# Even frequency classes from gathered rows of U, x copies on GpSimd, and earlier loads in the last pair

## The chip, the cores and the metric

The kernel runs on one NeuronCore of a Trainium2 chip. The metric is the device time of one execution in microseconds (us). TensorE, VectorE, ScalarE, GpSimd and SyncE appear in the profile as PE, DVE, ACT, POOL and SP; PEld is TensorE's weight load.

## The reference

Eight sequences x of 5696 rows and 128 channels are convolved with a filter h along the rows (by a Fourier transform of length 2S = 11392). The result goes through a spectral mix: of its transform of length S the lowest 64 modes are multiplied by complex 128x128 matrices, turned back and added; then u + relu(u @ w_ch) is returned.

```
L = 2 * S
y = irfft(rfft(x, n=L, axis=1) * rfft(h, n=L, axis=0), n=L, axis=1)[:, :S, :]
X = rfft(y, axis=1);  Xm = X[:, :64]
Y[:, :64] = einsum('bmd,mde->bme', Xm, w_r + 1j*w_i)
u = y + irfft(Y, n=S, axis=1)
out = u + maximum(u @ w_ch, 0)
```

## The kernel before, in words

A row number is written as 64 q + p, with q from 0 to 88 and p from 0 to 63. A transform over q (`a_tile`, 32 tiles a pair) gives 90 frequency classes k (`NK`) for each p; a second one over p within each class (`second`) gives 64 frequencies of the long transform per class, real and imaginary parts on the 128 partitions. Batches are worked in four pairs, g_ from 0 to 3 (`NP`). Pairs 1 and 2 are called the middle pairs here.

The classes of a pair are worked in 23 ticks of four (`NT`, `KT`; `tick`, L619). In tick t:

- PE makes the second transform of tick t into two PSUM banks. In pairs 1 to 3 an odd tick makes its own and the next one's (`twin`, L564).
- ACT copies the two banks to SBUF as f16 (`copied`, L557, tile Xs), and DVE multiplies them with the filter's transform Hs to U (`products`, L586). U holds the two products of both batches, 2048 elements a partition, in three rooms used in turn (`NU`). In a straight tick (`straight`, L567: t % 4 == 3 after pair 0) DVE reads PSUM itself, and ACT makes no copy.
- Two ticks later (`LC`) PE turns U of tick t-2 back over p with the constant matrices W1 and W2, in two halves, ACT evacuates each to Z, and SP stores Z to DRAM (zscr, 256 KB).
- Three ticks later (`LM`) PE adds up the low modes from Z of tick t-3 in PSUM bank 7 (`MB`): for each class and batch a matmul with Z as weights and a slice of the constant G as moving operand. An odd class gives all 128 mode rows, an even one two or four columns only, because frequency 2m of the long transform is mode m of the short one.

Z has 6 rooms in pair 0, 10 in pairs 1 and 2, and 8 in the last (`NZS`); a store that has not landed keeps its room. Meanwhile GpSimd issues loads of the next pair's x (`x_load`, L353, eight pieces, one every second tick, into the space that As has left), and DVE copies each into the padded tile Xin (`x_place`, L360). After the ticks come the evacuation of the modes (L696 to L699) and the remaining a_tiles of the next pair, whose first six are woven into the last ticks (`border`) and which need all eight pieces of Xin.

In the last pair GpSimd issues what the last stage needs, at ticks listed in `early` (L529): the mixing weights W in four pieces, two constants (S4, IB), and the stored Z of the first blocks (ZT0 to ZT2). Then the mix, and per block of rows: the back transform over the classes (matmuls on ZT), the modes' part (IBs, C), evacuation to UT, the product with WI = [w_ch, identity], relu (L831), addition (L832) and the store.

The order on each engine is the order in which the program records its operations (`Recorder.add`, L55). Waits follow from tokens: `reads` wait for a token's writer, `writes` and `after` for its writer and its readers. A transfer stands in the queue of the engine that issues it (`dma`, L316), and each ring has so many transfers in flight at once.

Of the kernel before, what the change touches and what calls it, by code (L numbers as in the profile page):

```python
# [4 lines left out]
P = 128  # L5
# [118 lines left out]
def bass_long_conv_fft__then__afno_spectral_mix_kernel(nc, x, h, moe_w_r, moe_w_i, moe_w_ch, out):  # L124
# [12 lines left out]

    qq = np.arange(NQ)
    pp = np.arange(J)
    kk = np.arange(NK)  # L140
    fwd = np.exp(-2j * np.pi * np.outer(qq, kk) / (2 * NQ))
    f1 = np.zeros((P, 2 * NK))
    f1[0:NQ] = np.stack([fwd.real, fwd.imag], axis=2).reshape(NQ, 2 * NK)
    mat = np.exp(-2j * np.pi * (pp[:, None, None] * kk[None, :, None] / L + pp[:, None, None] * pp[None, None, :] / J))
    strip = np.stack([-mat.imag, mat.real, mat.imag], axis=2).reshape(J, NK * 3 * J)
    MW = NK * 3 * J + J
    mt = np.zeros((P, MW))
    mt[0:J, 0:NK * 3 * J] = strip
    mt[J:P, J:MW] = strip
    th = 2.0 * np.pi * np.outer(pp, pp) / J  # L150
    c, s = np.cos(th), np.sin(th)
    w1 = np.block([[c, s], [-c, -s]])
    w2 = np.block([[-s, c], [-s, c]])
# [25 lines left out]
    for k in range(0, NK, 2):  # L179
# [2 lines left out]
        ge += [g[:, k, ri * M + m] for m in ms for ri in range(2)]  # L182
        at_e += 2 * len(ms)
    assert at_e == P
    g = np.concatenate([np.stack(ge, axis=1)] + [g[:, k] for k in range(1, NK, 2)], axis=1)

    def const(name, a):
# [6 lines left out]
    c_ib = const("cIB", ib.reshape(P, -1)[:, 0:SH])  # L194
    c_sg = nc.inline_tensor(np.ascontiguousarray(sg.astype(np.float32)), name="cSG")
    c_g = const("cG", g)
    wd = nc.dram_tensor("wscr", [P, 2 * M * D], F16, kind="Internal")
    zs = nc.dram_tensor("zscr", [NP * NK * P, 2 * D], F16, kind="Internal")

# [26 lines left out]
    a_g = take(HW * 2)  # L226
    g_sb = at("G", GW, F16, a_g)
    ah_sb = at("Ah", HW, F16, a_g)
    NU, NXS, NZ, NZX = 3, 2, 6, 10
    NZS = [NZ] + [NZX] * (NP - 2) + [8]  # L230
    NZL = NZS[-1]
    a_st = take((2 * NU + NXS + NZ) * 2048)
    h_in = at("Hin", J * D, F16, a_st)
# [5 lines left out]
    XB = XN * D  # L239
    x_all = at("Xr", 2 * XC * XB, F16, a_h)  # L240
    x_st = [at(f"Xt{i}", XB, F16, a_as + i * XB * 2) for i in range(2 * XC)]
    u_s = [at(f"U{i}", 2048, F16, a_st + i * 4096) for i in range(NU)]
    x_s = [at(f"Xs{i}", 1024, F16, a_st + NU * 4096 + i * 2048) for i in range(NXS)]
    z_s = [at(f"Zs{i}", 1024, F16, a_st + NU * 4096 + (NXS + i) * 2048) for i in range(NZ)] + \
          [at(f"Zt{i}", 1024, F16, a_g + GW * 2 + i * 2048) for i in range(NZX - NZ)]
# [1 line left out]
    wc_sb = at("Wc", 2 * P, F16, take(2 * P * 2))  # L247
    sg_sb = at("SG", 3, F32, take(12))
    XTW = 3 * M
    xt = at("XT", B * XTW, F16, a_g + GW * 2 + 2048 * (NZX - NZ))  # L250
    assert GW * 2 + 2048 * (NZX - NZ) + B * XTW * 2 <= HW * 2

    ZB = 16
    NC = 5
# [35 lines left out]
        return bass.AP(ps, p0 * 4096 + bank * 512 + off, [[4096, n]] + [list(d) for d in dims])  # L290

    R = Recorder(nc)
    for name, n in (("c", 16), ("x", 26), ("z", 8), ("w", 16), ("t", 10), ("s", 8), ("o", 12), ("p", 16), ("q", 10)):
        R.ring(name, n)

    def bank(i):
# [60 lines left out]
                bass.AP(x.tensor, x.offset + (2 * g_ + b) * S * D + q0 * J * D + c_ * XB, [[J * D, n], [1, XB]]),  # L357
                "x", (), [toks[p_]], after=after)

    def x_place(i, src, toks):  # L360
        R.add("vector", lambda e: e.tensor_copy(bass.AP(x_sb, i * XN * XS, [[XW, NQ], [XS, XN], [1, D]]),  # L361
                                                src),
              list(toks) + XZ, [("xin", i)])

    def w_pieces():
        out_ = []
# [124 lines left out]
    M_ALL = [("m", i) for i in range(MP)]  # L491
    G_ALL = [("g", i) for i in range(NG)]
    WT = [("w", i) for i in range(4)]
    ZY = [("zs", i, b) for i in range(NZL, NZX) for b in range(2)]
    ZX = [("zs", i, b) for i in range(NZ, NZL) for b in range(2)]
    zt_old = [(AST, AST), (AST, AST), (H_ALL, H_ALL), (H_ALL, H_ALL), (M_ALL[3:6], G_ALL)]

# [24 lines left out]
    def load_s4(part):  # L522
# [3 lines left out]

    V, A = "vector", "scalar"
    border = {NT - 1: [(0, 0, V)], NT: [(1, 2, V), (2, 0, V)], NT + 1: [(3, 2, A), (4, 0, V)], NT + 2: [(5, 2, V)]}
    early = {0: lambda: load_id(), 1: lambda: load_w(0), 3: lambda: load_w(1), 6: lambda: load_w(2), 8: lambda: load_w(3),  # L529
             12: lambda: load_s4(1), 16: lambda: load_s4(0),  # L530
             14: lambda: clear_zt(0),
             15: lambda: load_zt(0, "gpsimd"),
             NT - 2: lambda: (load_ib(), load_zt(1, "gpsimd", SLACK), load_zt(2, "gpsimd"), clear_zt(1), clear_zt(2))}
    pace = []
    SLACK = [("zd", NP - 1, s_) for s_ in range(NT - NZL)]

# [27 lines left out]
    def twin(g_, t):  # L564
        return g_ > 0 and t % 2 == 1

    def straight(g_, t):  # L567
        return g_ > 0 and t % 4 == 3

    def slot_of(g_, t):  # L570
        if g_ == 0 or t == 0:
            return XSLOT[(t + 1) % 2 if t and not with_h_at(g_, t) else 0]
        return XSLOT[((t - 1) // 4 + t) % 2]

    def second(g_, t):
        sl = slot_of(g_, t)
# [9 lines left out]
    def products(g_, t, sl):  # L586
        n = len(ticks[t])
        bk = [bank(sl), bank(sl + 1)]
        i = t % NU
        hv = bass.AP(h_sb, KT * t * D, [[2 * HW, P], [HW, 2], [0, 2], [1, n * D]])  # L590
        uv = bass.AP(u_s[i], 0, [[2048, P], [1024, 2], [512, 2], [1, n * D]])
        src = pv(sl, 0, [[0, 2], [512, 2], [1, n * D]])
        if t == 0:
            e = turns("e", list(range(NXS)))
            evac(bass.AP(x_s[e], 512, [[1024, P], [1, n * D]]), pv(sl + 1, 0, [[1, n * D]]), [bank(sl + 1)], [("xs", e)], eng="scalar")
            hv = bass.AP(h_sb, 0, [[2 * HW, P], [HW, 2], [1, n * D]])
            for b, s_, tok in ((0, pv(sl, 0, [[0, 2], [1, n * D]]), bank(sl)),
                               (1, bass.AP(x_s[e], 512, [[1024, P], [0, 2], [1, n * D]]), ("xs", e))):
                R.add("vector", lambda e, b=b, s_=s_: e.tensor_tensor(bass.AP(u_s[i], b * 512, [[2048, P], [1024, 2], [1, n * D]]), s_, hv, MULT),  # L599
                      [tok, ("h", t, 0), ("h", t, 1, 0), ("h", t, 1, J)], [("u", i)])  # L600
            return
        if not straight(g_, t):
            e = onchip.get((g_, t))
            if e is None:
                e = copied(g_, t, sl)
            src, bk = bass.AP(x_s[e], 0, [[1024, P], [0, 2], [512, 2], [1, n * D]]), [("xs", e)]
        R.add("vector", lambda e: e.tensor_tensor(uv, src, hv, MULT),  # L607
              bk + [("h", t, 0), ("h", t, 1, 0), ("h", t, 1, J)], [("u", i)])

    Z_OLD = [("ag", k) for k in range(NS, NS + 8 * (NZX - NZ))]  # L610
    XPLACE = [9, 10, 12, 15, 16, 18, 20, 22], [9, 10, 13, 14, 17, 18, 20, 22]

    def zroom(g_, s_):
        return (s_ - 2 * NZ) % NZX if g_ == 0 and s_ >= 2 * NZ else s_ % NZS[g_]
# [1 line left out]
    def xtok(n):  # L616
        return [("xt", n, p_) for p_ in range(2)]

    def tick(g_, t):  # L619
        if g_ + 1 < NP:  # L620
            for i in range(2 * XC):
                if t == XPLACE[g_ > 0][i]:
                    x_place(i, bass.AP(x_st[i], 0, [[XB, NQ], [D, XN], [1, D]]), xtok(i))
        with_h = with_h_at(g_, t)
        if t < NT:
            of_two = t > 0 and twin(g_, t - 1)
# [8 lines left out]
        if drain and t >= NT:  # L635
            j, sl, e = drain.pop(0)
            a_tile(j, [sl], e)
        if g_ + 1 < NP and t % 2 == 0 and 0 < t <= 4 * XC:
            i = t // 2 - 1
            x_load(g_ + 1, i, x_st[i], xtok(i), [("u", t % NU)] + AST)  # L640
        if LC <= t < NT + LC:
            s_ = t - LC
            n = len(ticks[s_])
            i, zi = s_ % NU, zroom(g_, s_)
            zb = [turns("z", ZBANK) for b in range(2)]
            for b in range(2):
                for r in range(2):
                    mm(pv(zb[b], 0, [[1, n * D]]), (W1, W2)[r], u_s[i][:, r * 1024 + b * 512:r * 1024 + b * 512 + n * D],
                       r == 0, r == 1, [("u", i), ("wc",)], [bank(zb[b])])
                evac(bass.AP(z_s[zi], b * D, [[1024, P], [2 * D, n], [1, D]]),  # L650
                     pv(zb[b], 0, [[D, n], [1, D]]), [bank(zb[b])], [("zs", zi, b)], eng="scalar",
                     after=once(("zx", zi, b), Z_OLD) if zi >= NZ else ())
            zo = (g_ * NK + KT * s_) * P * 256
            dma("sync", bass.AP(zs, zo, [[256, P], [P * 256, n], [1, 256]]),
                bass.AP(z_s[zi], 0, [[1024, P], [256, n], [1, 256]]), "z",
                [("zs", zi, 0), ("zs", zi, 1)], [("zd", g_, s_)])
            if drain and t >= NT:
                j, sl, e = drain.pop(0)
                a_tile(j, [sl], e)
        if LM <= t < NT + LM:  # L660
            s_ = t - LM
            zi = zroom(g_, s_)
            for i, k in sorted(enumerate(ticks[s_]), key=lambda q: (s_ > 0 or q[1] != 1, q)):
                for b in range(2):
                    if k % 2:
                        o, off, n, sl = pv(MB, b * P, [[1, P]]), (k + 1) // 2 * P, P, (k + 1) // 2
                    else:
                        ms, off = even[k]
                        n, sl = 2 * len(ms), 0
# [17 lines left out]
    for g_ in range(NP):  # L687
        for t in range(NT + LM):
# [4 lines left out]
            if g_ == NP - 1 and t in early:  # L693
                pace[:] = [("u", min(t, NT - 1) % NU)]
                early[t]()
        evac(bass.AP(xt, 2 * g_ * XTW + M, [[B * XTW, P], [XTW, 2], [1, P]]), pv(MB, 0, [[P, 2], [1, P]]),  # L696
             [bank(MB)], [("xt", g_)], 1.0 / 64, eng="scalar", after=[("ag", k) for k in range(NS + 2 * XN, NK)])
        evac(bass.AP(xt, 2 * g_ * XTW, [[B * XTW, P], [XTW, 2], [1, M]]), pv(MB, M, [[P, 2], [1, M]]),
             [bank(MB)], [("xtn", g_)], -1.0 / 64, eng="vector" if g_ + 1 == NP else "scalar", after=[("ag", k) for k in range(NS + 2 * XN, NK)])  # L699
        if g_ + 1 < NP:  # L700
            for j in range(6, 32):
                a_tile(j, [(4, 6, 0, 2)[(j - 7) % 4] if j > 6 else 0], "both" if j == 31 else V if j % 2 else A)
                if j == 31:
                    keep(8, 6)
                if wp and j % 2 == 1:
                    dst, src_, ring, tok = wp.pop(0)
                    dma("gpsimd", dst, src_, ring, (), [tok], after=[("as", j)])
# [189 lines left out]
```

## Time and profile before

| what | value |
|---|---|
| median of 3 runs | 392.7 us (392.68 to 393.31) |
| the profiled execution | 392.87 us, span 390.6 us, granted TensorE clock 0.982 |
| PE busy | 364.1 us, 93% of the span |
| ACT busy | 311.2 us, 80% |
| DVE busy | 301.9 us, 77% |
| POOL busy | 85.6 us, 22% |
| ticks of pair 1 / pair 2 / pair 3 begin | 109.35 / 164.78 / 220.91 us |
| a_tiles after pair 1 / pair 2 | about 152 to 164.7 / 208 to 220.8 us |

The span is the time from the first to the last instruction of one execution. Busy shares are means over stages with different limits, so the prediction reads single stages. "A <- B: 1.8" in a view of waits says that engine A stood idle for 1.8 us until B released it.

### The profile page before, as it was taken

Reading aid. Unit: us, or ns where it says so; the run is one execution under the profiler, and the core shown is the slowest. Engines: PE = TensorE matmul, PEld = TensorE weight load, DVE = VectorE, ACT = ScalarE, POOL = GpSimd, SP = SyncE. Lnnn points to the kernel's source line nnn. Section 1 sums busy time; section 2 is a strip of 40 time slices with the busy share of each in tenths; the row PEclk is TensorE's granted clock in tenths of the full one; section 3 lists DMA queues with packets and bytes.
Section 4 is the critical chain, followed back from the end, with each engine's and each line's share of the span. In section 5 each row is a group of like instructions: output and inputs, shape, how many; then the busy total and the mean of one; then the engine's idle time right before and its main releaser. Section 6 shows DMA issues by size and latency. Waiting matters only on the chain.

```text
span 390.6 us, 12485 instructions
## 1 busy us (share of the span) xinstructions
PE 364.1 (93%) x5346; PEld 281.3 (72%) x5346; DVE 301.9 (77%) x346; ACT 311.2 (80%) x489; POOL 85.6 (22%) x134
## 2 busy tenths in 40 slices
PE   7799899998989999999989899989989999999992
PEld 7698766665866667856657666658878988988871
DVE  3369889987998998989998988754437767677784
ACT  8289689997989997899997899984447676777783
POOL 8600022210643210823213210319200000000000
PEclk9899999999999999999999999996999999999998
DMA  7998569998899995999995689999999999998766
GB/s 146 178 283 337 138 126 297 274 251 251 92 135 201 238 268 169 127 136 231 245 261 111 64 264 351 298 354 379 406 388 393 414 407 412 410 399 356 305 274 273
DMA packets 87090, 103.94 MB, mean 266 GB/s; under 512 B 22824, under 2 KB 72616, under 8 KB 83564
## 3 DMA queue, kind: packets, MB, share of 16 engines
q1 hardware_dynamic: 62523, 67.73, 49.7%
q0 software_dynamic: 24512, 35.43, 43.6%
q8 instruction: 42, 0.69, 0.7%
q14 instruction: 13, 0.10, 0.1%
HBM read 70.61 MB, written 51.12 MB: 312 GB/s over the span
## 4 chain that ended last, share of the span: by engine, by line
PE 63%; DMA 15%; DVE 8%; ACT 6%; issue 3%; POOL 3%; SPq 0%; POOLq 0%; DVEq 0%
PE ps L320 63%; DMA ZT4b<-zscr 4%; DMA zscr<-Zt 3%; DMA Hs<-Hs 3%; DMA Hin<-in_h_dram 3%; DMA Xt<-in_x_dram 2%; DVE As L314 2%; DVE U L599 2%; ACT As L310 2%; DVE U L607 1%; DVE Xin L361 1%; ACT UT L308 1%; ACT Zs L308 1%; DVE Hs L312 1%; ACT Xs L308 1%
## 5 line engine op out<-in xcount | busy, mean ns | idle before, releaser
L607 DVE TENSOR_TENSOR U<-Xs,Hs 128x2048 f16<-128x2048 f16 (+1 forms) x73 | 86.9, 1192 | 15.1 <-ACT Xs L308 11.0
L320 PE MATMUL ps<-U,Wc 128*128 128x512 f16 (+1 forms) x368 | 94.0, 376 | 1.3 <-DVE U L607 0.8
L308 ACT CAST Xs<-ps 128x1024 f16<-128x1024 f32 (+1 forms) x77 | 74.7, 974 | 11.9 <-PE ps L320 6.8
L308 ACT CAST Zs<-ps 128x512 f16<-128x512 f32 (+1 forms) x134 | 70.6, 595 | 2.7 <-PE ps L320 2.4
L832 DVE TENSOR_TENSOR O<-ps,R 128x512 f32<-128x512 f32 x81 | 52.5, 685 | 19.8 <-ACT R L831 12.5
L831 ACT ACTIVATE R<-ps 128x512 f32<-128x512 f32 x96 | 50.9, 572 | 16.3 <-PE ps L320 15.8
L314 DVE TENSOR_SCALAR As<-ps 128x720 f16<-128x720 f32 x70 | 57.7, 884 | 5.4 <-PE ps L320 4.8
L320 PE MATMUL ps<-F,Xin 128*128 128x180 f16 x512 | 53.7, 249 | 3.6 <-DVE Xin L361 2.3
L320 PE MATMUL ps<-As,M 64*128 64x128 f16 x1440 | 50.5, 217 | 3.5 <-DVE U L599 2.9
L320 PEld LDWEIGHTS ps<-F,Xin 128*128 128x128 f16 x512 | 44.4, 155 | 12.1 <-DVE Xin L361 2.8
L320 PE MATMUL ps<-WI,UT 128*128 128x256 f16 x360 | 51.8, 279 | 0.5 <-DVE O L832 0.4
L320 PEld LDWEIGHTS ps<-U,Wc 128*128 128x128 f16 x368 | 28.7, 97 | 30.3 <-ACT Zs L308 4.4
L310 ACT ACTIVATE As<-ps 128x720 f16<-128x720 f32 (+1 forms) x61 | 45.7, 770 | 5.7 <-PE ps L320 4.3
L317 POOL DMA_DIRECT2D Xt<-in_x_dram x48 | 26.0, 546 | 101.0 <-PE ps L320 97.1
L320 PEld LDWEIGHTS ps<-As,M 64*128 64x128 f16 x1440 | 40.6, 94 | 9.9 <-DVE U L599 3.6
L308 ACT CAST UT<-ps 128x712 f16<-128x712 f32 x40 | 30.0, 752 | 18.7 <-PE ps L320 17.7
L320 PEld LDWEIGHTS ps<-WI,UT 128*128 128x128 f16 x360 | 39.3, 152 | 4.2 <-issue 1.9
L320 PE MATMUL ps<-IBs,C 128*128 128x356 f16 x128 | 40.5, 326 | 0.6
L320 PEld LDWEIGHTS ps<-G,Zs 128*128 128x128 f16 x524 | 26.6, 96 | 14.9 <-ACT Zs L308 2.2
L607 DVE TENSOR_TENSOR U<-ps,Hs 128x2048 f16<-128x2048 f32 x15 | 34.3, 2283 | 0.0
L320 PE MATMUL ps<-G,Zs 128*128 128x128 f16 (+2 forms) x524 | 33.0, 192 | 0.1
L312 DVE CAST UT<-ps 128x712 f16<-128x712 f32 x24 | 21.4, 890 | 11.0 <-PE ps L320 11.0
(87 smaller groups left out, 509.8 us busy)
## 6 DMA issues: line engine op xcount, KB each, us to landing
out_dram<-O SPq DMA_DIRECT2D x39, 512.0 KB, 8.7
zscr<-Zs SPq DMA_DIRECT2D x64, 256.0 KB, 7.4
Xt<-in_x_dram POOLq DMA_DIRECT2D x24, 320.0 KB, 7.3
zscr<-Zt SPq DMA_DIRECT2D x24, 256.0 KB, 7.3
W<-wscr POOLq DMA_DIRECT2D x4, 1024.0 KB, 9.1
M<-cM POOLq DMA_DIRECT2D x5, 720.0 KB, 20.6
ZT0a<-zscr SPq DMA_DIRECT2D x3, 1024.0 KB, 13.1
Hs<-Hs SPq DMA_DIRECT2D x44, 64.0 KB, 6.3
```

Of the source, the lines that this page charges most:

```text
L308: R.add(e, lambda h_: h_.copy(dst, src), reads, writes, after=after)
L310: R.add(e, lambda h_: h_.activation(dst, src, COPY, scale=scale), reads, writes, after=after)
L312: R.add(e, lambda h_: h_.tensor_copy(dst, src), reads, writes, after=after)
L314: R.add(e, lambda h_: h_.tensor_scalar_mul(dst, src, scale), reads, writes, after=after)
L317: R.add(eng, lambda h_: h_.dma_start(dst, src), reads, writes, ring=ring, after=after)
L320: R.add("tensor", lambda h_: h_.matmul(o, l, r, start=st, stop=sp), reads, writes)
L361: R.add("vector", lambda e: e.tensor_copy(bass.AP(x_sb, i * XN * XS, [[XW, NQ], [XS, XN], [1, D]]), src), list(toks) + XZ, [("xin", i)])
L599: R.add("vector", lambda e, b=b, s_=s_: e.tensor_tensor(bass.AP(u_s[i], b * 512, [[2048, P], [1024, 2], [1, n * D]]), s_, hv, MULT), [tok, ...
L607: R.add("vector", lambda e: e.tensor_tensor(uv, src, hv, MULT), bk + [("h", t, 0), ("h", t, 1, 0), ("h", t, 1, J)], [("u", i)])
L831: R.add("scalar", lambda e: e.activation(rv, src_r, RELU), bk, [("r", i % NR)], after=once(("r", i % NR), G_ALL + XTT + [("y", 0), ("y", 1 ...
L832: R.add("vector", lambda e: e.tensor_tensor(ov, src_u, rv, ADD), bk + [("r", i % NR)], [key + (h_,)], after=once(key, old))
```

## The change

1. In the middle pairs the even classes no longer go through matmuls with G. The two frequencies of an even class that are wanted, j = 0 and j = 63 of the 64, are single rows of U (real and imaginary parts; the rows 32 and 63 are swapped in the constants, so that the rows lie on partitions 0 and 64, or 0, 32, 64 and 96). For each tick SP stores these rows of U to a DRAM tile `es` (`even_rows`: 2 or 4 partitions, 8 runs of 256 B from each), recorded behind the store of Z of the tick before. In the a_tile stage SP loads all 66 rows back, with a constant selection matrix (`even_load`, at a_tile 8), into Z rooms 7 and 0; eight matmuls of 128 columns sum them, DVE adds the result to the modes, and ACT writes the negated copy (`even_modes`, at a_tile 27).
2. U has four rooms in the middle pairs instead of three; the fourth takes the place of two Z rooms. Pairs 1 to 3 have 8 Z rooms.
3. In the middle pairs the straight ticks are 3 and every odd tick from 7 to 21, instead of 3, 7, 11, 15 and 19. The eight copies of x into Xin run on GpSimd at the ticks 7, 9, ... 21, each after the product of the tick before (token `dv`); x loads are issued at odd ticks from 1 instead of even ticks from 2.
4. In the last pair the loads of W are issued in ticks 0, 1, 2 and 4 instead of 1, 3, 6 and 8, S4b in tick 8 instead of 12, and IB in tick 10 instead of 21.

```diff
+    jj = np.arange(J)
+    jj[[J // 2, J - 1]] = J - 1, J // 2
...
-    NU, NXS, NZ, NZX = 3, 2, 6, 10
-    NZS = [NZ] + [NZX] * (NP - 2) + [8]
+    NU, NXS, NZ, NZX, NZT = 3, 2, 6, 8, 10
+    NUS = [NU] + [NU + 1] * (NP - 2) + [NU]
+    NZS = [NZ] + [NZX] * (NP - 1)
...
-    early = {0: lambda: load_id(), 1: lambda: load_w(0), 3: lambda: load_w(1), 6: lambda: load_w(2), 8: lambda: load_w(3),
-             12: lambda: load_s4(1), 16: lambda: load_s4(0),
+    early = {0: lambda: (load_id(), load_w(0)), 1: lambda: load_w(1), 2: lambda: load_w(2), 4: lambda: load_w(3),
+             8: lambda: load_s4(1), 10: lambda: load_ib(), 16: lambda: load_s4(0),
...
-             NT - 2: lambda: (load_ib(), load_zt(1, "gpsimd", SLACK), load_zt(2, "gpsimd"), clear_zt(1), clear_zt(2))}
+             NT - 2: lambda: (load_zt(1, "gpsimd", SLACK), load_zt(2, "gpsimd"), clear_zt(1), clear_zt(2))}
...
+    XP0 = 7
     def straight(g_, t):
-        return g_ > 0 and t % 4 == 3
+        if g_ + 1 < NP:
+            return g_ > 0 and t % 2 == 1 and (t >= XP0 or t == 3) and t + 1 < NT
+        return t % 4 == 3
...
+    def even_rows(g_, t):
+        i = t % NUS[g_]
+        p_, s_, row, to = (2, J, 4 * TB + t, TA) if t < TA else (4, J // 2, t - TA, TB)
+        dma("sync", bass.AP(es, (g_ * ER + row) * 8 * D, [[to * 8 * D, p_], [1, 8 * D]]),
+            bass.AP(u_s[i], 0, [[s_ * 2048, p_], [2 * D, 8], [1, D]]), "e", [("u", i)], [("es", g_, t)])
+    def even_load(g_):
+        dma("sync", z_s[EC][0:ER, 0:4 * P], c_sel.ap(), "e", (), [("ev", 1)], after=EZT)
+        dma("sync", z_s[EZ][0:ER, :], bass.AP(es, g_ * ER * 8 * D, [[8 * D, ER], [1, 8 * D]]), "e",
+            [("es", g_, t) for t in range(NT)], [("ev", 0)], after=EZT)
+    def even_modes(g_, sl):
+        for b in range(2):
+            for n in range(2):
+                for r in range(2):
+                    mm(pv(sl, b * P, [[1, P]]), z_s[EZ][0:ER, ((2 * r + b) * 2 + n) * D:((2 * r + b) * 2 + n + 1) * D],
+                       z_s[EC][0:ER, (2 * n + r) * P:(2 * n + r + 1) * P], (b, n, r) == (0, 0, 0), (b, n, r) == (1, 1, 1),
+                       [("ev", 0), ("ev", 1)] + EZT, [bank(sl)])
+        xv = bass.AP(xt, 2 * g_ * XTW + M, [[B * XTW, P], [XTW, 2], [1, P]])
+        R.add("vector", lambda e: e.tensor_tensor(xv, pv(sl, 0, [[P, 2], [1, P]]), xv, ADD), [bank(sl), ("xt", g_)], [("xt", g_)])
...
     def tick(g_, t):
         if g_ + 1 < NP:
             for i in range(2 * XC):
-                if t == XPLACE[g_ > 0][i]:
-                    x_place(i, bass.AP(x_st[i], 0, [[XB, NQ], [D, XN], [1, D]]), xtok(i))
+                if t == (XP0 + 2 * i if g_ else XPLACE[i]):
+                    x_place(i, bass.AP(x_st[i], 0, [[XB, NQ], [D, XN], [1, D]]), xtok(i),
+                            "gpsimd" if g_ else "vector", [("dv", g_, t - 1)] if g_ else ())
...
-        if g_ + 1 < NP and t % 2 == 0 and 0 < t <= 4 * XC:
-            i = t // 2 - 1
-            x_load(g_ + 1, i, x_st[i], xtok(i), [("u", t % NU)] + AST)
+        if g_ + 1 < NP and 0 < t <= 4 * XC and t % 2 == (g_ > 0):
+            i = (t - 1) // 2
+            x_load(g_ + 1, i, x_st[i], xtok(i), [("u", t % NUS[g_])] + AST)
...
+            for q in range(0 if t == LC else t - 1, min(t, NT)) if gathers(g_) else ():
+                even_rows(g_, q)
...
+                    elif gathers(g_):
+                        continue
...
+                if j == 8 and gathers(g_):
+                    even_load(g_)
+                if j == JE and gathers(g_):
+                    even_modes(g_, (4, 6, 0, 2)[(j - 6) % 4])
```

## The prediction

> **What bounds the kernel now.** I read the page's slices first (PE 9 tenths nearly everywhere), then the chain that ended last, to find the stages, and then the busy time of each engine in stretches of four ticks of a middle pair, since an average over the span says little here. A line gives the stretch, its length, and the busy us (and instructions) of PE, PEld, DVE, ACT, POOL, then the granted clock, the busy share of the DMA engines and GB/s.
>
> ```profile
> 182.80:189.80 7.00, 7.00 (x118) 4.53 (x114) 6.91 (x6) 6.86 (x12) 2.08 (x4) 1.00 1.10 262
> ...
> 196.90:203.90 7.00, 6.61 (x102) 4.06 (x95) 6.38 (x6) 6.86 (x13) 0.00 (x0) 1.00 1.06 256
> ```
>
> Four things are full at once in the first: PE, DVE, ACT, and the DMA engines, whose packets overlap (share over 1). The timeline gives the pace: PE begins the second transforms of two ticks at 179.06, 182.54, 186.10, 189.58 and 193.14, so four ticks take 7.04 us, 1.76 each.
>
> ```profile
> 183.94 2.28 DVE L607 TENSOR_TENSOR U<-ps,Hs 128x2048 f16<-128x2048 f32 x1
> ...
> 186.14 1.22 DVE L607 TENSOR_TENSOR U<-Xs,Hs 128x2048 f16<-128x2048 f16 x1
> ...
> 187.27 0.69 DVE L361 COPY Xin<-Xt 89x2048 f16<-89x2048 f16 x1
> ...
> 187.88 1.23 DVE L607 TENSOR_TENSOR U<-Xs,Hs 128x2048 f16<-128x2048 f16 x1
> ```
>
> The starts show what each one really costs, as records overlap by 0.08: a straight product 2.20 (183.94 to 186.14), a product from the copy 1.13 (186.14 to 187.27), an x copy 0.61. ACT's copies cost about 0.98 and its two evacuations of a tick about 1.0.
>
> Then the transfers, by size and time to landing: the whole run, then the window 165 to 208.
>
> ```profile
> zscr<-Zs SPq DMA_DIRECT2D x64, 256.0 KB, 7.4
> ...
> Hs<-Hs SPq DMA_DIRECT2D x44, 64.0 KB, 6.3
> ```
>
> ```profile
> zscr<-Zs SPq DMA_DIRECT2D x14, 256.0 KB, 8.6
> ```
>
> A swap of a quarter of a store's size takes nearly as long: on SP's queue a small transfer waits for the large ones ahead of it. Stores issued at 176 to 186 landed after 9.8 to 11.4 us, those at 203 to 209, with no x load left, after 1.8 to 4.6.
>
> The end of the run has two waits that the change touches, in the waits of 260 to 290:
>
> ```profile
> PE ps L320 <- DMA ZT4b<-zscr: 1.8, 1, 1.8
> ...
> PE ps L320 <- ACT Zt L308: 0.9, 1, 0.9
> ```
>
> **The change, part by part, on the profiled execution** (span 390.6 of 392.87, so 2.27 lies around it; the median of the runs is 392.7, 0.17 less; I add the sum to 392.7).
>
> *Engines in the middle pairs.* Ticks 1 to 6 keep their straight products (tick 3); from 7 to 22 every second tick is straight instead of every fourth. Two such ticks now cost 3.52. After: DVE 2.20 + 1.13 = 3.33 with the x copies gone to GpSimd; ACT 0.98 + 2 x 1.0 = 2.98; PE loses four of the eight matmuls of a modes block. The starts 180.94 to 181.26 and 182.12 to 182.54 give such a block 0.32 to 0.42 us; the four gone are worth between nothing and half of it, and I take half, 0.19 a tick, as each has a weight load of its own: 3.52 - 0.37 = 3.15. So DVE is the next bound, at 3.33: 0.19 less for each of 8 twin ticks, **-1.5 us a pair**, if nothing else binds.
>
> *Gather stores.* Each tick, SP issues a transfer that reads 2 or 4 rows of U, behind the store of the tick before. What waits for it: product t+4, which rewrites the same of the four rooms. Behind that product on DVE stand all later products, and W1/W2 on PE wait for those. The time allowed: in pair 2 the product of tick 10 ends at 184.03, the store of tick 9 is issued at 185.67 and takes SP 0.36 at the least, and the product of tick 14 starts at 189.84, so the gather has 189.84 - 186.03 = 3.8 us. No row shows such a gather. Bounds: 1.8 (a store on an idle queue) costs nothing; 6.3 (the swaps) is 2.5 late, 8.6 (stores) 4.8 late. A late product delays the gather issued after it, so lateness adds once in five ticks, some 3.2 times over the 16 ticks with x loads: 0, 8.0 or 15.4 us a pair, if the queue stayed as long. It doesn't: a slower pace lets it drain, down to the pace that the DMA engines can hold. That I take, as the share over 1 shows queueing that feeds itself. Work: 1.76 x 1.07 = 1.88 us of engine time a tick. A packet of SP's queue between 113 and 143 took 41.8% x 16 x 30 us / 7393 = 27 ns; a gather is 16 or 32 runs of 256 B. If they ride on few engines, 8 on each, these have 0.22 more: (1.88 + 0.22) / 1.07 = 1.96 us a tick, 0.20 over today's. 16 x 0.20 = 3.2, less 0.57 for the three twin ticks after it at DVE's pace: **+2.6 us a pair**. Spread over all engines it is 0.03 to 0.05 a tick, and the pair loses about 0.1 by work alone; the queue ahead of the gather is then still there.
>
> The Trainium skill, "DMA: Bandwidth & Descriptors", section "Why a DMA increments its semaphore by 16 and not by 1", says that the slowest dimension sets how many engines carry a transfer, so 2 rows would ride on 2. Its section on queues, rings and completion order says that each engine consumes its ring in order. By both the gather stands behind the store on the few engines it has, the dearer of my two cases; without them the sum would be some 5 us less. The trace agrees with the second rule (swaps 6.3 beside stores 7.4), and nothing in it shows the first.
>
> *x copies on GpSimd*, 16 of them, each released by the product before a straight one. The nearest row is POOL's memset of 2048 elements a partition, 1.82 us (L508); DVE's own copy took 0.68. The straight product beside it lasts 2.20, so a copy of 1.8 to 2.1 is hidden: nothing. Behind it on POOL stand the next two x issues (2 x 0.53), which wait for the straight product anyway, and there is room: 2.1 + 1.06 against 3.33. The last copy starts with tick 21 instead of 22, and the loads are issued a tick sooner; PE waited 0.3 and 1.0 for Xin at the two borders, and this goes: **-1.3**. Late next there is As by DVE, as today.
>
> The Trainium skill, "SBUF — State Buffer", section "Who interferes with whom", says that GpSimd's reads and a VectorE instruction with two SBUF inputs exclude each other for a whole instruction. By it a copy that outlasts the straight product holds the next product back by the excess; by the row there is none. No run here shows such a copy.
>
> *Even modes at the end of a pair.* 8 matmuls of 128 columns (217 ns records, about 0.06 apart) on PE, one addition of 256 columns on DVE (between 0.29 and 0.69 by L314 and L312 rows), in a stage where DVE is busy 12.15 of 12.6 us and PE 11.99. The two loads are issued with a_tile 8, and 19 tiles at 0.41 pass before they are read; the pieces of w that move in this stage landed in 4.5. Cost 0.5 a pair: **+1.0**. Eight Z rooms instead of ten: a room comes back after 8 ticks, 14.1 us, above every landing in the middle pairs (11.4 at most): nothing.
>
> *Last pair's loads.* The DMA share is 0.61 in 220.9 to 234.9 and over 1 from then to 288. W is issued 2 to 7 us sooner, S4b four ticks and IB (734 KB, 1.8 us at 394 GB/s) eleven ticks sooner, into that gap. So ZT4b lands about 2 sooner, and its wait of 1.8 goes. The 0.9 for a Z room may go, but the stores behind W reached 11.6 us and may get longer, against 14.1. I take **-2.0**, bounds -2.7 and +1.
>
> Sum: 2 x 2.6 - 1.3 + 1.0 - 2.0 = +2.9: **395.6 us**.
>
> **Rivals.**
>
> 1. *The gathers land in time* (not slower). If they go past the stores, or the x loads leave their engines free, DVE's 3.33 holds: 2 x -1.5 - 1.3 + 1.0 - 2.0 = -5.3, **387.4**. It decides from a landing of 3.8 us. For it: 1.8 on an idle queue; against: 6.3 and 8.6.
> 2. *Gathers in time, but PE or ACT frees nothing* (the change doesn't do what it says: the small matmuls were covered by weight loads). The pace stays 3.52: -1.3 + 1.0 - 2.0 = -2.3, **390.4**.
> 3. *The copy on GpSimd becomes the bound.* If it takes half again the memset, 2.7, and starts 0.2 late, the next product on DVE is 0.7 late, 16 times: 11.2 on top of rival 1, **398.6**. For it: no row of a POOL copy; against: 1.82.
> 4. *Loss and gain cancel*: the gathers are late only while the queue is longest, +1.2 a pair: 2.4 - 2.3 = +0.1, **392.8**.
>
> **Chances.** Forecast 0.50 (its own range 393.8 to 399.5, the upper end by the swaps' 8.0 a pair over somewhat more than half of the ticks), rival 1 0.22, rival 2 0.10, rival 3 0.12, rival 4 0.06. A measurement tells 0.2%, 0.8 us, from no change. Faster: rivals 1 and 2 and a little of the forecast's foot, 0.34; within it 0.08; slower 0.58. The range leaves about a tenth on each side: 387.2 to 400.5; the dearest bound (15.4 a pair) lies outside, since it needs a queue that doesn't drain.
>
> **What would show it.** Forecast: DVE U waits for a DMA of es from U in ticks 5 to 18 of both middle pairs, twin ticks of 3.7 to 4.0 us there and 3.3 to 3.4 after, es landing in 4 to 6 us. Rival 1: es landing under 3.8, DVE without gaps, twin ticks of 3.3. Rival 3: POOL Xin over 2.3 us, and products from Xs starting late or longer than 1.23. Last pair: the wait for ZT4b gone. I would be wrong above all if the gathers' engines are not the crowded ones.

## The result, and the profile after

| | before | after |
|---|---|---|
| median | 392.69 us (391.44 to 393.31, 4 runs) | 417.77 us (415.14 to 418.68, 4 runs) |
| profiled execution, its span | 392.87, 390.6 | 418.68, 416.8 |
| granted TensorE clock | 0.982 | 0.965 |

The ratio is 1.068 (95% interval 1.063 to 1.074): 25 us slower, where +2.9 was forecast and the range ended at 400.5. Some executions of a kernel take over 1.5% longer than its fastest; the ratios, and the medians of the experiments below, leave these slow ones out. Stage by stage on the profiled executions, cut where each pair's first product starts, where the next pair's a_tiles start and where the mix starts:

| stage | before | after | difference |
|---|---|---|---|
| start to the products of pair 0 | 45.48 | 45.71 | +0.2 |
| pair 0 with its a_tiles | 64.51 | 66.94 | +2.4 |
| ticks of pair 1 / of pair 2 | 38.43 / 39.14 | 48.36 / 48.55 | +9.9 / +9.4 |
| a_tiles and tick 0 behind pair 1 / pair 2 | 17.00 / 16.99 | 18.58 / 18.40 | +1.6 / +1.4 |
| ticks of pair 3 | 42.81 | 43.43 | +0.6 |
| mix to the end | 126.27 | 126.87 | +0.6 |

The +2.4 of pair 0 is not the change's: its ticks are the same code, and in the runs below, where they are the same too, this stage took from 63.6 to 67.7 us. About three quarters of the loss lie in the ticks of the middle pairs. The stretches, before and then after, with columns as in the prediction:

```profile
109.99:148.42 38.43, 37.07 (x589) 23.63 (x583) 36.52 (x32) 37.05 (x60) 8.87 (x17) 1.00 1.06 219
165.42:204.56 39.14, 37.06 (x589) 23.62 (x583) 36.61 (x32) 37.51 (x60) 9.96 (x18) 1.00 1.05 215
```

```profile
112.65:161.01 48.36, 38.28 (x508) 22.19 (x503) 35.89 (x23) 34.12 (x56) 24.03 (x25) 0.96 0.91 179
179.59:228.14 48.55, 39.13 (x509) 22.72 (x504) 36.18 (x24) 33.79 (x55) 23.95 (x25) 0.93 0.88 174
```

DVE and ACT have less work than before, as forecast, and PE 80 matmuls fewer; yet no engine is full any more. The waits of the whole run say why (engine, awaited, us in total, times, longest):

```profile
DVE U L633 <- DMA escr<-U: 19.5, 9, 4.4
PEld ps L342 <- DVE U L633: 19.5, 9, 3.7
PE ps L342 <- DVE U L633: 17.8, 8, 3.5
```

DVE stands before a product whose room of U a gather store (escr<-U) still reads, and PE stands behind DVE. The timeline of DVE in pair 1 (start, length of all joined, in brackets the idle time before), first at ticks 3 to 7 and then at ticks 11 to 13:

```profile
116.95 2.28 DVE L633 TENSOR_TENSOR U<-ps,Hs 128x2048 f16<-128x2048 f32 x1
123.64 3.53 DVE L633 TENSOR_TENSOR U<-Xs,Hs 128x2048 f16<-128x2048 f16 x3 [4.41 <-DMA escr<-U]
128.01 2.29 DVE L633 TENSOR_TENSOR U<-ps,Hs 128x2048 f16<-128x2048 f32 x1 [0.84 <-PE ps L342]
...
138.29 2.28 DVE L633 TENSOR_TENSOR U<-ps,Hs 128x2048 f16<-128x2048 f32 x1
140.49 1.22 DVE L633 TENSOR_TENSOR U<-Xs,Hs 128x2048 f16<-128x2048 f16 x1
141.62 2.28 DVE L633 TENSOR_TENSOR U<-ps,Hs 128x2048 f16<-128x2048 f32 x1
```

Unstalled, a twin tick takes 141.62 - 138.29 = 3.33 us, exactly as worked out. But six stalls of 1.2 to 4.4 us stand in the two pairs, at ticks 4, 10 or 11, and 17 of each, with three of 0.3 to 0.5 beside them. The chain through pair 1 has three gathers in it (start, us):

```profile
117.18 6.37 DMA escr<-U
...
131.25 5.80 DMA escr<-U
...
148.22 7.26 DMA escr<-U
```

And the stores of Z in the ticks of pair 2 (window 179.59 to 228.14), to be set beside the 8.6 of before:

```profile
zscr<-Zs SPq DMA_DIRECT2D x16, 256.0 KB, 5.0
```

### The profile page after: what moved, and what is told of

It reads as the page before. It is cut to its first block, busy times and chain, and to the rows that moved or that the text cites. A ratio compares the mean times of both kernels' runs of the same rounds, so it can differ in the third digit from the quotient of the medians.

```text
span 416.8 us, 12170 instructions
## 1 busy us (share of the span) xinstructions
PE 367.8 (88%) x5182; PEld 277.9 (67%) x5182; DVE 303.3 (73%) x332; ACT 304.5 (73%) x481; POOL 114.9 (28%) x150
## 4 chain that ended last, share of the span: by engine, by line
PE 49%; DMA 19%; DVE 15%; ACT 9%; issue 6%; POOL 1%; SPq 0%; DVEq 0%; ACTq 0%; POOLq 0%
PE ps L342 49%; DMA escr<-U 9%; DVE As L336 6%; DMA zscr<-Zs 6%; DVE U L633 5%; ACT Zs L330 3%; DMA Hin<-in_h_dram 2%; ACT As L332 2%; DMA Hs<-Hs 2%; DVE U L625 2%; ACT Xs L330 2%; ACT R L902 1%; ACT UT L330 1%; ACT Zt L330 1%; DVE Hs L334 1%
## 5 line engine op out<-in xcount | busy, mean ns | idle before, releaser
L342 PE MATMUL ps<-U,Wc 128*128 128x512 f16 (+1 forms) x368 | 99.1, 386 | 11.7 <-DVE U L633 9.1
L633 DVE TENSOR_TENSOR U<-Xs,Hs 128x2048 f16<-128x2048 f16 (+1 forms) x65 | 77.0, 1191 | 25.9 <-DMA escr<-U 10.5
L330 ACT CAST Xs<-ps 128x1024 f16<-128x1024 f32 (+1 forms) x69 | 66.5, 969 | 35.9 <-PE ps L342 26.8
L330 ACT CAST Zs<-ps 128x512 f16<-128x512 f32 x150 | 80.2, 600 | 10.5 <-PE ps L342 6.3
L903 DVE TENSOR_TENSOR O<-ps,R 128x512 f32<-128x512 f32 x81 | 52.6, 684 | 20.4 <-ACT R L902 11.7
L342 PE MATMUL ps<-As,M 64*128 64x128 f16 x1440 | 52.5, 220 | 12.9 <-DVE U L633 8.7
L633 DVE TENSOR_TENSOR U<-ps,Hs 128x2048 f16<-128x2048 f32 x23 | 52.6, 2286 | 14.1 <-DMA escr<-U 9.0
L342 PEld LDWEIGHTS ps<-As,M 64*128 64x128 f16 x1440 | 41.6, 96 | 20.4 <-DVE U L633 9.7
L342 PEld LDWEIGHTS ps<-WI,UT 128*128 128x128 f16 x360 | 39.2, 152 | 4.2 <-issue 1.9
L342 PE MATMUL ps<-G,Zs 128*128 128x2 f16 (+2 forms) x452 | 34.3, 204 | 0.1
L383 POOL COPY Xin<-Xt 89x2048 f16<-89x2048 f16 x16 | 30.4, 1900 | 14.2 <-DVE U L633 14.2
```

Source lines behind the costliest of these rows:

```text
L330: R.add(e, lambda h_: h_.copy(dst, src), reads, writes, after=after)
L342: R.add("tensor", lambda h_: h_.matmul(o, l, r, start=st, stop=sp), reads, writes)
L383: R.add(eng, lambda e: e.tensor_copy(bass.AP(x_sb, i * XN * XS, [[XW, NQ], [XS, XN], [1, D]]), src), list(toks) + XZ, [("xin", i)], after= ...
L903: R.add("vector", lambda e: e.tensor_tensor(ov, src_u, rv, ADD), bk + [("r", i % NR)], [key + (h_,)], after=once(key, old))
```

## The experiments

Theory at the start: DVE's product waits for its room, and the room for a gather store that lands late. What makes it late was open: its place behind the stores in SP's queue, its own packets, or the engines' other traffic. Rivals: the copies on GpSimd, the new straight ticks, the loss of two Z rooms. For each kernel the median, and the ratio to the kernel before, which was run again beside it, with the 95% interval. Code cuts are marked by "...".

**No gathers** (the even classes go through matmuls with G again; all the rest of the change stays).

```diff
 def gathers(g_):
-    return NUS[g_] > NU
+    return False
```

> The changed kernel, but the even classes go through the matmuls with G again: no gather stores, no loads of them, no even_modes; four rooms of U, eight of Z, copies of x on GpSimd, the new straight ticks and the early loads stay. Room theory (product t+4 waits until the gather that reads its room of U has landed; 19.5 us of DVE idle time in the changed kernel): the ticks of a middle pair fall from 48.4 us to 38 to 39.5, no DVE wait for escr is left, 391 to 395 us in all. Rival, copies and straight ticks (the stalls come from GpSimd's copies and the longer DVE work, and the transfer is only what is named): the ticks stay above 44 us a pair, the whole above 407.

Measured: 390.97 us, 0.998 (0.995 to 1.001); ticks of 38.2 and 38.3 us a pair, and no wait on a gather. The whole loss hangs on the gathers; without them copies on GpSimd, straight ticks and Z rooms cost nothing.

**Five rooms of U** in the middle pairs, six of Z there.

```diff
-    NUS = [NU] + [NU + 1] * (NP - 2) + [NU]
-    NZS = [NZ] + [NZX] * (NP - 1)
+    NUS = [NU] + [NU + 2] * (NP - 2) + [NU]
+    NZS = [NZ] + [NZ] * (NP - 2) + [NZX]
...
```

> The changed kernel with five rooms of U in the middle pairs instead of four, and six of Z there (eight in the last pair as before). Room theory: a gather has about 1.7 us more to land, 5.5 instead of 3.8, against landings of 5.5 to 7 us; DVE's waits for escr fall from 19.5 us to 4 to 11, the time to 402 to 411 us. Rival, work (the gathers load two or four of the sixteen engines, and these set the pace): the waits come later but the pace is the same, 415 to 419 us.

Measured: 400.7 us, 1.026 (1.017 to 1.035), from two runs of 402.52 and 398.95. One more room gives back 17 of 25 us: it is the time that a room is held.

**Small gather**: one run of 256 B for each row instead of eight; seven eighths of the gathered rows are left out.

```diff
-        dma("sync", bass.AP(es, (g_ * ER + row) * 8 * D, [[to * 8 * D, p_], [1, 8 * D]]),
-            bass.AP(u_s[i], 0, [[s_ * 2048, p_], [2 * D, 8], [1, D]]), "e", [("u", i)], [("es", g_, t)])
+        dma("sync", bass.AP(es, (g_ * ER + row) * 8 * D, [[to * 8 * D, p_], [1, D]]),
+            bass.AP(u_s[i], 0, [[s_ * 2048, p_], [1, D]]), "e", [("u", i)], [("es", g_, t)])
...
```

> The changed kernel with one run of 256 B from each partition in every gather instead of eight; the other seven eighths of the gathered rows are left out, and even_modes sums the first run in their place. Room theory (a gather lands late because it stands in the queue behind the stores and between the x loads, not because of its own work): waits for escr 16 to 20 us, 414 to 419 us. Rival, work: an eighth of the pieces on those engines, so the waits fall below 10 us and the time below 408.

Measured: 410.31 us, 1.048 (1.040 to 1.055); the waits are 15.5 us in 9 instead of 19.5. Both ranges are missed: the time lies between them, the waits 0.5 us under the first. The gather's own size is the lesser part: in the changed kernel 3.7 of its 4.5 us (medians) pass before its first packet.

**Early loads alone**: the kernel before with the new table `early` and nothing else.

> The kernel before with only the table of the last pair's loads changed (W in ticks 0, 1, 2, 4, S4b in 8, IB in 10). As predicted: the wait for ZT4b goes, 390.7 us. By the changed kernel's trace (first stores of the last pair landed after 13 to 15 us, a stall of PE of 2.8 us in the mix): 392.7 to 394.5 us.

Measured: 391.59 us, 0.999 (0.995 to 1.003). In the profile the wait for ZT4b is gone and the mix to the end takes 123.59 us, 2.7 less than before, with 0.3 more in pair 3's ticks. The time lies between the two that were expected. The gain is real in its stage and too small to show in medians that vary by 1%.

**No x loads**: neither the loads of x nor its copies in the middle pairs (pairs 2 and 3 work on the x of pair 1).

```diff
-                if t == (XP0 + 2 * i if g_ else XPLACE[i]):
+                if g_ == 0 and t == XPLACE[i]:
...
-        if g_ + 1 < NP and 0 < t <= 4 * XC and t % 2 == (g_ > 0):
+        if g_ == 0 and 0 < t <= 4 * XC and t % 2 == 0:
```

> The changed kernel with the x loads and the x copies of the two middle pairs left out (so pairs 2 and 3 work on the x of pair 1, and the output is not the reference's); the gather stores stay. Theory A (the gather stores land late because SP's queue and the DMA engines also carry the x loads of every odd tick, 0.85 MB a pair): with them gone the gathers land within a twin tick, DVE's waits on escr fall from 19.5 us to under 4, a middle pair's ticks from 48.4 to under 40, total under 400 us. Theory B (the gathers are late because of their place behind the big stores of their own tick, x loads or not): waits stay over 10 us, ticks over 44 a pair, total 408 to 415. Between the two: both count.

Two things in that text are wrong: the x loads are on GpSimd's queue, not SP's, and they are 712 packets of 4096 B a pair, 2.9 MB. Measured: 391.36 us, 1.002 (0.999 to 1.006), with all gathers in place and no wait on any:

```profile
108.96:145.79 36.83, 35.70 (x508) 21.09 (x503) 35.55 (x24) 33.16 (x55) 0.51 (x1) 1.00 0.63 155
164.26:201.09 36.83, 35.68 (x509) 21.08 (x504) 35.53 (x24) 33.17 (x55) 0.90 (x2) 1.00 0.56 148
```

So theory A. The stores of Z are still ahead of each gather, and it lands in 1.4 us all the same. The run leaves out GpSimd's copies too; that the loads are what counts, the changed kernel shows within one run. In ticks 0 to 16, with x loads in flight, its gathers take 4.8 us from issue to their last packet; in ticks 17 to 22, behind the same stores and with copies still running, 1.7. Between a gather's issue and its first packet 84 packets of 4096 B of GpSimd's queue are on their way on average in ticks 0 to 16, about the 89 rows of one piece of x, and none from tick 18 on.

**Gathers on ACT's queue.**

```diff
-        dma("sync", bass.AP(es, (g_ * ER + row) * 8 * D, [[to * 8 * D, p_], [1, 8 * D]]),
+        dma("scalar", bass.AP(es, (g_ * ER + row) * 8 * D, [[to * 8 * D, p_], [1, 8 * D]]),
```

> The changed kernel with the gather stores issued from ACT's queue; nothing else moved. Theory A (the place in SP's order and in SP's queue makes them late: they are issued behind two 512 KB tick stores whose ZscR waits hold SP, and their packets stand behind those stores' packets): a gather is issued as soon as ACT comes to it and lands in some 2 to 4 us, the waits on escr fall from 19.5 to under 8, total 395 to 405; ACT pays its own price of at most 26 issues. Theory B (the DMA engines are busy, whichever queue it comes from): landing stays 5 to 7 us, total 412 to 418.

A tick's store is 256 KB, not the 512 KB of that text.

**Gather first**: on SP the gather of tick t-1 goes ahead of the store of tick t-2.

```diff
+            for q in range(0 if t == LC else t - 1, min(t, NT)) if gathers(g_) else ():
+                even_rows(g_, q)
             dma("sync", bass.AP(zs, zo, [[256, P], [P * 256, n], [1, 256]]),
...
-            for q in range(0 if t == LC else t - 1, min(t, NT)) if gathers(g_) else ():
-                even_rows(g_, q)
```

> The changed kernel with the gather store of tick t-1 recorded on SP ahead of the Z store of tick t-2 instead of behind it. Theory A (the place behind that store is what costs): the gather then stands behind one store less and lands some 1.9 us sooner, the price of a tick's own DMA work; the waits on escr fall from 19.5 to 5 to 10 us and the total to 402 to 410. If it is not the place in the order (theory B, the queue as a whole), within 2 us of the changed kernel's 417.8.

Measured: 402.53 us, 1.029 (1.023 to 1.034), and 402.51 us, 1.029 (1.024 to 1.033). The waits, of ACT's queue and of gather first:

```profile
DVE U L633 <- DMA escr<-U: 5.5, 10, 2.3
```

```profile
DVE U L633 <- DMA escr<-U: 6.2, 10, 1.7
```

Theory A foresaw the waits in both, but for a reason that is half wrong: with x loads in flight the landing stays at 4.3 and 4.8 us, even in a queue with no store in it, where a gather's first packet still comes 3.5 us after its issue (ticks 0 to 16). What fell is the time from the end of the product to the issue, from 1.54 us to 0.47 and 0.06. The Trainium skill, "DMA: Bandwidth & Descriptors", section "Queues, rings and completion order", says that each DMA engine goes round the queues and drains a whole packet of some 9 to 17 descriptors before it changes. The trace fits this: one record of an x load takes 324 ns in the median and some over 1100, so eleven of them in a row, or fewer, make up the 3.5 us that the gather waits in a queue of its own. That they do is not shown: the trace does not tell the engines apart.

**No gathers, old rooms**: as the first, with 3 rooms of U and 6, 10, 10 and 8 of Z.

> The changed kernel without the gathers (even classes by matmuls again) and with the old rooms (3 of U, 10 of Z in the middle pairs, 8 in the last); twelve straight products, GpSimd's copies of x, the x loads at odd ticks and the earlier loads of the last pair stay. Theory: its time is that of before less what the earlier loads give (2.7 us from the mix to the end, by the run with those alone), and the other parts give a middle pair at most 0.5 us: 388 to 391.5 us. If the rooms mattered to the run without gathers, it is faster than that one's 391.0; if the fewer turned products gain nothing because TensorE sets the tick, the same within 0.3%.

Measured: 391.90 us, 1.003 (1.000 to 1.006), 0.4 above the range and not better than before. Its ratio is 0.5% above that of the first run, and the intervals touch: a difference by the rooms is not shown.

**Fewer warming matmuls** (`WARM = 60` instead of 92, at the start of the program). It was made for the 3.1 us that the mix lost. PE in the mix of the changed kernel, and then here:

```profile
292.82 1.26 PE L342 MATMUL ps<-XT,W 128*128 128x16 f16 x36
296.88 0.82 PE L342 MATMUL ps<-XT,W 128*128 128x16 f16 x22 [2.80 <-issue]
```

```profile
284.97 1.12 PE L342 MATMUL ps<-XT,W 128*128 128x16 f16 x32 [0.20 <-issue]
285.93 0.20 PE L342 MATMUL ps<-S4a,ZT0a 128*128 128x89 f16 x1
```

> The changed kernel with 60 instead of 92 warming matmuls at the very start (they compute nothing that is used). It shifts TensorE's list of instructions by 64 entries against the places where new instructions are fetched. Theory: the 2.8 us in which TensorE stands still in the mix, waiting for nothing, beside a 16 KB packet of the instruction queue, is such a fetch; then the stall leaves the mix (7.5 us becomes 4.5 to 5) or moves to another place of the program. Rival: it comes from the data of the mix; then it stays where it is, between 2 and 3 us long.

Measured: 409.14 us in a single run. The mix takes 4.47 instead of 7.54 us, and PE waits "on issue" for no more than 0.2 us at a time anywhere. The Trainium skill, "Runtime: NRT & Kernel Launch", section "Instruction fetch mechanics", has instructions fetched in blocks of 16 KB, at a cost that is mostly hidden. A packet of 16384 B of the instruction queue starts at 294.50, within the stall of 294.08 to 296.88. PE stands still at this place for 0.7 to 3.2 us in all eight traces that have gathers and 92 warming matmuls, and in none of the other eight, whose matmuls ahead of the mix are 32 fewer or 164 more. So it hangs on the place in PE's list of instructions; that the fetch is the cause, and was not hidden here, is inferred from the packet and from this shift.

**Gather first and five rooms**, then the same **with 60 warming matmuls**.

> The changed kernel with both repairs: the gather store of tick t-1 ahead of the Z store of tick t-2, and five rooms of U in the middle pairs (6 of Z there, 8 in the last pair). Theory (a room is held for the delay of the issue and the landing, 0.06 and 4.2 us with the gather first, and five rooms allow a tick of 1.67 us more than four): no wait on escr is left over 1 us in all, a middle pair's ticks take 36.5 to 38 us, the a_tile stages stay at 16.6, total 389 to 394. Rival (DMA engines set the pace of the early ticks themselves): ticks over 39 a pair, total over 396.

> The kernel with both repairs (gather store first, five rooms of U) and 60 warming matmuls instead of 92. Theory: as the one with both repairs, less the stall of 2.2 to 2.8 us in the mix if that is a fetch of instructions that has moved to a harmless place: 387 to 392. Rival: the stall only moves elsewhere on the path, or fewer warming matmuls leave the clock lower at the start: no difference or slower by up to 1 us.

Measured: 396.88 us, 1.021 (1.014 to 1.029), and 393.32 us, 1.007 (1.004 to 1.009). The waits on gathers fall to 3.6 and 2.6 us, here the second:

```profile
DVE U L633 <- DMA escr<-U: 2.6, 8, 0.6
```

The first misses its 389 to 394, and its ticks of 39.3 and 39.1 us lie where its rival begins; of the 2.4 us a pair that they are above those without x loads, the waits on gathers are 1.8. The second misses its 387 to 392; it is the best kernel with gathers and all loads, and still a little slower than before. Its ticks take 38.7 and 38.4 us, its mix to the end 123.5, its a_tile stages 18.6 and 18.8 against 17.0 (the 16.6 of the expectations is a shorter cut of this stage).

**x loads in halves** on the changed kernel, and with all repairs: 2 KB a row in two transfers each.

```diff
-            x_load(g_ + 1, i, x_st[i], xtok(i), [("u", t % NUS[g_])] + AST)
+            x_load(g_ + 1, i, x_st[i], xtok(i), [("u", t % NUS[g_])] + AST, 0 if g_ else None)
+        if 0 < g_ < NP - 1 and 0 < t <= 4 * XC and t % 2 == 0:
+            i = (t - 2) // 2
+            x_load(g_ + 1, i, x_st[i], [k + (1,) for k in xtok(i)], [("u", (t - 1) % NUS[g_])] + AST, 1)
...
```

> The changed kernel with each x load of the middle pairs in two halves of 2 KB a row, one at the odd tick as before, one a tick later; nothing left out, the same bytes. Theory A (a gather lands late because one x load holds the DMA engines for a burst of some 2 us, with packets of 330 to 1000 ns): landing falls from 4.8 us in the early ticks to 3 to 4, the waits on escr from 19.5 to 8 to 14, total 405 to 412. Theory B (only the bytes count): within 3 us of the changed kernel's 417.8. If the doubled number of issues on GpSimd (16 more a pair) delays the x copies, it is slower than that.

> The kernel with the gather store first, five rooms of U, 60 warming matmuls and the x loads of the middle pairs in halves of 2 KB a row; nothing left out. Theory: what is left of the waits on escr (2.6 us in the run without the halves) goes, so that a middle pair's ticks fall from 38.7 and 38.4 to 37 to 37.8 us, near the 36.8 of the run without x loads; the a_tile stages stay at 16.6, since nothing in them is changed: 390 to 393 us. Then the predicted gain of the engines is real and the a_tile stages give it back. Rival: the ticks stay at 38 to 39, because the DMA engines, with a share of over 1 in the ticks with x loads, hold the stores of Z as well: 392.5 to 395.

Measured: 406.80 us, 1.040 (1.033 to 1.046), and 396.88 us, 1.018 (1.012 to 1.023). The same bytes in packets of 2 KB (173 ns in the median instead of 324): the gathers land in 3.9 us in both, instead of 4.8 in the changed kernel, the waits are 7.0 us on the changed kernel, and none is left with all repairs. The halves did not come a tick apart, though: GpSimd issued all four transfers in one row, so it is shorter packets that this shows. And with all repairs the ticks took 40.1 us. DVE's products from Xs in pair 1, without the halves and then with them (busy us, mean ns):

```profile
L633 DVE TENSOR_TENSOR U<-Xs,Hs 128x2048 f16<-128x2048 f16 x12 | 14.9, 1241 | 2.1 <-ACT Xs L330 1.2 <-DMA escr<-U 0.8
```

```profile
L634 DVE TENSOR_TENSOR U<-Xs,Hs 128x2048 f16<-128x2048 f16 x12 | 18.0, 1497 | 1.2 <-ACT Xs L330 1.2
```

GpSimd and DVE in that run:

```profile
131.65 2.07 POOL L339 DMA_DIRECT2D Xt<-in_x_dram  x4
133.71 1.90 POOL L384 COPY Xin<-Xt 89x2048 f16<-89x2048 f16 x1
```

```profile
132.73 2.28 DVE L634 TENSOR_TENSOR U<-ps,Hs 128x2048 f16<-128x2048 f32 x1
134.93 1.77 DVE L634 TENSOR_TENSOR U<-Xs,Hs 128x2048 f16<-128x2048 f16 x1
```

The copy starts 0.98 us into the straight product, ends at 135.61, and the product from 134.93 on lasts 0.55 longer than 1.22, which is about what is left of the copy. The straight product (one input in PSUM) and the copy keep their times. The Trainium skill, "SBUF — State Buffer", section "Who interferes with whom", says that a VectorE instruction with two SBUF inputs and GpSimd's reads exclude each other; the trace agrees, with 1.77 against 1.22. This is the third rival of the prediction, with another trigger: late issues, not a slow copy.

**Two runs of 2 KB in one transfer**, all else as with 60 warming matmuls.

> As the run with all repairs, but each x load of the middle pairs remains one transfer and only its rows are written as two runs of 2 KB, so that GpSimd issues no more transfers than in the changed kernel. Theory from the run with all repairs: there no wait on escr was left, and the ticks took 40.1 us a pair only because GpSimd's copies started behind two more issues and the VectorE product beside their end took up to 2.04 instead of 1.22 us; with the issues gone the products are back at 1.21 to 1.4, the ticks at 37 to 38 a pair, total 389 to 392.5. Rival: the transfer is still made of 4 KB packets; then it repeats the run without halves, 392 to 394.5, with packets of 4096 B in the trace. If packets are of 2 KB and products stay at 1.5 or more, the issues are not the cause.

Measured: 394.42 us, 1.011 (1.006 to 1.015). The packets stayed at 4096 B, so it repeats the kernel with both repairs and 60 warming matmuls; products were at 1.21 to 1.31 again, ticks at 39.4 and 38.0. The range is missed, and the rival's 392 to 394.5 with 4096 B holds. Short packets without the added issues were thus not tried.

The holds side by side: a room of U is held from the end of its product to the last packet of its gather, read from the packets of 256 B in SP's (or ACT's) queue.

| kernel | product end to issue | issue to last packet, ticks 0-16 / 17-22 | held, mean (longest) | waits on gathers | ticks, pair 1 / 2 |
|---|---|---|---|---|---|
| changed | 1.54 us | 4.8 / 1.7 us | 5.5 (9.4) us | 19.5 us | 48.4 / 48.6 us |
| ACT's queue | 0.47 | 4.3 / 2.5 | 4.3 (7.3) | 5.5 | 43.2 / 39.2 |
| gather first | 0.06 | 4.8 / 2.4 | 4.3 (7.7) | 6.2 | 41.8 / 41.5 |
| first, five rooms, 60 | 0.14 | 5.3 / 2.8 | 4.8 (7.3) | 2.6 | 38.7 / 38.4 |
| no x loads | 1.80 | 1.4 / 1.5 | 3.2 (4.1) | 0 | 36.8 / 36.8 |

At the pace of 3.33 us a twin tick, four rooms allow a hold of 2 x 3.33 less the product's own 2.20 or 1.13: 4.5 or 5.5 us. Five allow 6.7. Where the hold stays below, no wait is seen; where its long cases go over, DVE waits.

## Why the prediction was wrong, point by point

1. *Engines in the middle pairs*, -1.5 a pair. Right: twin ticks of 3.33 us where nothing stalls, and ticks of 36.8 us without x loads, 1.6 and 2.3 under before. With x loads and both repairs that is eaten by the rest of the waits (1.3 us a pair) and by products drawn out beside copies (38.7 and 38.4).
2. *Gather stores*, +2.6 a pair. **The step that failed.** Measured against the ticks without x loads it is 48.4 - 36.8 and 48.6 - 36.8: 11.5 and 11.7 a pair, of which 10.2 and 9.4 are DVE's waits; the rest, 1.3 and 2.3, goes with PE at a lower clock (last section) and was not taken apart. The mechanism, the place (DVE's product four ticks later) and even the landing ("4 to 6 us") were right. So was most of the size that I had and gave up: 3.2 late gathers of 2.5 us, 8.0 a pair; it was three long waits a pair of 3.1 us on average. What I put in its place was wrong: "It doesn't: a slower pace lets it drain, down to the pace that the DMA engines can hold." It did drain. Stores landed in 5.4 and 5.0 instead of 7.5 and 8.6 us and the DMA share fell from 1.06 and 1.05 to 0.91 and 0.88, yet a gather still took 4.8. Its delay does not come from a queue that builds up over many ticks (the gathers of tick 0 took 5.9 and 5.5 already; with the gather first they were issued ahead of the x load, and took 1.4 and 1.3) but from the x load of its own twin tick, 89 packets that every twin tick brings anew, whatever the pace. The reading of the swaps, that a small transfer on SP's queue waits for the large ones ahead of it, does not hold either: without x loads a gather behind the same stores lands in 1.4. A rate (engine time a tick) was used where a latency (issue plus landing against the rooms' slack) decides; the bounds 8.0 and 15.4 should have stayed within the range.
3. *Allowed time.* 3.8 us from issue was near: 4.5 or 5.5 from the product's end, less an issue delay of 1.54, is 2.9 or 4.0.
4. *Copies on GpSimd*, nothing. Right in the changed kernel: 1.90 us each (1.82 was the row taken), and products beside them 1.31 at most. The cover is thin, as the run with all repairs shows.
5. *Waits for Xin*, -1.3. Too much, though in the changed kernel 1.4 us of PE's waiting became 0.4: there the ticks were 10 us longer, so a copy had time. With both repairs and 60 warming matmuls the waits are 0.6 and 0.4, so 1.0 is left.
6. *Even modes*, +0.5 a pair. Too low: the stages grew by 1.6 and 1.4. The addition on DVE (0.41) and eight matmuls (0.61) are as sized, but PE also waits for the bank that the addition frees, in the changed kernel:

```profile
PEld ps L342 <- DVE XT L671: 2.3, 2, 1.1
...
PE ps L342 <- DVE XT L671: 1.9, 2, 1.0
```

7. *Last pair's loads*, -2.0. Right alone (-2.7 + 0.3). In the changed kernel the 2.8 us stall of PE in the mix, which nothing in the trace of before announced, hides it; with 60 warming matmuls the mix to the end takes 122.3 to 123.8.
8. *Rival 1* (387.4 with gathers in time) did not happen even without x loads (391.4): the a_tile stages give back 1.5 a pair, the stall in the mix 2.0, and the ticks of pair 3 took 1.2 more.

## What to carry to other kernels

A small transfer that holds a buffer is priced by its latency in the traffic of its own few microseconds, not by the mean load of the DMA engines: take the landing of the nearest small transfer, add the delay of its issue, and set the sum against the slack of the rooms. Issue it first, and give it a room more than the sum needs; both together took back 21 of the 25 us, the issue order alone 15 and the room alone 17. When a bound has been worked out from rows, an argument that it will "drain" needs a row too, or the bound stays in the range.

## What the runs showed of the hardware that was not expected

- A transfer in a queue that carries nothing else still waits while another queue has packets: on ACT's queue 3.5 us to the first packet in ticks 0 to 16, 1.9 in ticks 17 to 22. On SP's queue, in the run without x loads, it was 1.25.
- Gathers ride on few engines. On ACT's queue stand, beside their 256 B packets, 66 packets of 4 B a pair (semaphore updates): one for each row of 13 gathers of 2 rows and 10 of 4. Over a pair SP's queue has 88 more of them in the changed kernel than in the run without gathers, these 66 and 11 for each of the two loads of 66 rows. The Trainium skill, "DMA: Bandwidth & Descriptors", section "Why a DMA increments its semaphore by 16 and not by 1", says that the slowest dimension sets the number of engines, and that each posts once; the trace agrees.
- Behind stops of PE of some microseconds the granted clock fell to half for 3.41 us, once in the ticks of pair 1 and twice in those of pair 2:

```profile
125.23:128.62 3.39, 3.39 (x40) 2.31 (x38) 2.55 (x3) 1.76 (x3) 2.08 (x3) 0.50 0.81 134
203.74:207.13 3.39, 3.39 (x19) 1.66 (x18) 2.28 (x2) 2.55 (x5) 2.27 (x2) 0.50 0.91 155
220.80:224.19 3.39, 3.39 (x25) 1.83 (x26) 2.85 (x2) 2.14 (x3) 1.89 (x1) 0.50 0.47 134
```

  They follow stops of 3.5, 2.5 and 2.8 us; two others of 3.1 and 3.2 us had none behind them, so these runs give no length at which it falls. With the gather first no stop in the ticks is over 1.7 us, and the clock stays at 1.00 there. The 508 and 509 matmuls were busy for 38.3 and 39.1 us, against 36.4 in the kernel with both repairs and 60 warming matmuls.
- A GpSimd copy of 89x2048 f16 takes 1.90 us (1.89 to 1.91), 2.8 times DVE's 0.68.
